# Casts, their remainders and the block differences of MLP 2 moved to other steps; the stores and weight sums of MLP 1 regrouped

## The chip, the cores and the metric

The kernel runs on one core of a Trainium2 chip. The metric is the device time of one execution in microseconds (us). The program has five instruction streams: TensorE (PE, with its weight loads shown apart as PEld), VectorE (DVE), ScalarE (ACT), GpSimd (POOL) and SyncE (SP). Each runs its own instructions strictly in their order; they meet at semaphores. A transfer is started by an instruction in one of these streams, and an instruction that waits there holds up all that stand behind it.

## The reference

```python
def reference(**kwargs):
    attn_out = _attn_ref(**attn_kwargs)      # 4 x 8 heads, 576 x 64, local and strided masks
    x = attn_out.transpose(0, 2, 1, 3).reshape(2304, 512)
    x = _moe_ref(x, w_in, w_out)             # MLP 1: h = x @ w_in; g = h * clip(h + 3, 0, 6) / 6; g @ w_out
    return _moe2_ref(x, w_in2, w_out2)       # MLP 2: h = x @ w_in2; g = max(h, 0) + log1p(exp(-|h|)); g @ w_out2
```

There are 2304 tokens of width 512, and the inner width of both MLPs is 2048. The weights come as float64.

## The kernel before, in words

**Numbers.** A float32 factor is split into a rounded part (`hi`, a cast by ACT) and the remainder (`lo`, a subtraction by DVE), both in the format that TensorE multiplies fast; a product is hi·hi + hi·lo + lo·hi, three matmuls. A block can't be multiplied before its cast and then its subtraction are done.

**Stages.** Attention is worked off in pieces beside MLP 1. MLP 1 runs over five chunks of tokens (`c`, one of 384 and four of 480) and 16 blocks of the inner width (`f`), 80 steps in all: `pe_h`, the activation on ACT and DVE (`post1`, `post2a`, `post2b`), and two steps later `pe_y`. At the end of a chunk `evac` copies four sums from PSUM into tiles `ysb` and stores them to `ydr` in DRAM (L781, L782). In chunk 0 the output weights are split and stored to `wdr` (`split_wout`, L151), and later chunks load them back (`load_split`, L157). The order of MLP 1's instructions is set by a scheduler.

**Preparing MLP 2's weights.** From chunk 1 on, each unit of four steps (16 units, numbered by `o` and `g`) loads two blocks of MLP 2's float64 weights (`prep_load`, one unit ahead), turns them into float32 (`w_scale` on ACT L116, `w_bits` on DVE L121 and L127), forms sums of blocks (`prep_sums`, DVE L198), splits the result (`prep_split`, ACT L216 and DVE L217 into tiles `so`, of which there are two) and stores it to `sdr` (L218): four casts, four subtractions and four stores per unit.

**MLP 2** multiplies 2 x 2 blocks with seven products in place of eight, so that sums and differences of blocks stand before and behind the products. It has three chunks of 768 tokens. A chunk has 56 steps of phase 1 (eight groups `g`, seven products `i` each, in a skewed order) and 56 of phase 2 (seven products in the order `ORDER2`, eight groups each); a step is six matmuls. The program order is the order written (`in_order()`); each step also issues one 256 KB weight load `su` (L859) on SP's queue, ten steps ahead. After a step of phase 1, `post_1` (L901 to L941) forms h on DVE (`vadd`, L866), the softplus on ACT (abs L932, exp L902, log L903) and its last step on DVE (`soft_end`, L897); two groups make a tile `gq`.

**The units of phase 2.** `t_unit(c, k)` makes one factor of phase 2 from a tile `gq`: for two of the seven products a block difference first (DVE L866, 768 columns), then the cast `th` (ACT L959) and the remainder `tl` (DVE L960). There are 28 units per chunk. Units 0 to 2 are written after the steps of product 2 of groups 3, 5 and 7 in phase 1, the others beside phase 2's steps, by the table `T_AT`; `X_AT` does the same for the next chunk's input (`x_split`, L821 and L822; `x_sums`, L810). `out_put` transposes a result on DVE (L970) before it is stored.

Of the kernel before, what the change touches and what calls it, by code (L numbers as in the profile page):

```python
# [7 lines left out]
F32 = mybir.dt.float32  # L8
# [8 lines left out]
P = 128  # L17
# [5 lines left out]
def attn_two_mlps(  # L23
# [120 lines left out]
    def split_wout(f):  # L144
        raw = words(1, 0, f, F32)[1]
        wst_t.pop((1, 0, f))
        hi, lo = sw_tile("woh"), sw_tile("wol")
        nc.scalar.copy(hi, raw)
        nc.vector.tensor_tensor(out=lo, in0=raw, in1=hi.bitcast(F32), op=ALU.subtract)
        for i, t in enumerate((hi, lo)):  # L150
            nc.sync.dma_start(out=wdr[f][i], in_=t.bitcast(F32))  # L151
        wo_t[0, f] = (hi, lo)
# [14 lines left out]

    def prep_f32(o, g):
        for f in (2 * g, 2 * g + 1):
            w_scale(o, 1, f)  # L170
        w_bits((o, 1, 2 * g), (o, 1, 2 * g + 1))

    def prep_parts(o, g, i):
# [8 lines left out]

    def prep_sums(o, g):
# [8 lines left out]
        for out_, x, y, op in (  # L192
            (s1, a21, a22, ALU.add),
            (s2, s1, a11, ALU.subtract),
            (s3, a11, a21, ALU.subtract),
            (s4, a12, s2, ALU.subtract),
        ):
            nc.vector.tensor_tensor(out=out_, in0=x, in1=y, op=op)  # L198

    def prep_split(o, g, i):  # L200
# [8 lines left out]
        for a, z, src in parts:  # L209
            t = wsl.tile([P, 2, 2, DH], F32R, tag="so", name="so")[:, : z - a]  # L210
            hi, lo = (t[:, :, j] for j in range(2))
            if o:
                hi, lo = (x.rearrange("p b (x m) -> p b m x", x=2) for x in (hi, lo))
                if a == 0:
                    src = src.rearrange("p b (m x) -> p b m x", x=2)
            nc.scalar.copy(hi, src)  # L216
            nc.vector.tensor_tensor(out=lo, in0=src, in1=hi.bitcast(F32), op=ALU.subtract)  # L217
            nc.sync.dma_start(  # L218
                out=sdr[o][g][4 * i + a : 4 * i + z].rearrange("b p n -> p b n"),
                in_=t.rearrange("p b j n -> p b (j n)").bitcast(F32),  # L220
            )
        wst_t.pop((o, 1, 2 * g + i))

# [641 lines left out]
    def vadd(out_, x, y, op=ALU.add):  # L865
        return nc.vector.tensor_tensor(out=out_, in0=x, in1=y, op=op)  # L866
# [80 lines left out]

    def t_unit(c, k):
        i, q = ORDER2[k // 4], k % 4
        g = g2_t[c, q]  # L950
        if i == 7:
            vadd(g[:, 0], g[:, 4], g[:, 0], ALU.subtract)
        elif i == 4:
            vadd(g[:, 1], g[:, 4], g[:, 1], ALU.subtract)
        hi, lo = (
            l2p["g"].tile([P, 2, HT], F32R, tag=f"t{n}", name=f"t{n}", bufs=5) for n in "hl"
        )
        raw = g[:, GI[i]]
        nc.scalar.copy(hi, raw)  # L959
        nc.vector.tensor_tensor(out=lo, in0=raw, in1=hi.bitcast(F32), op=ALU.subtract)  # L960
        tt[c, i, q] = (hi, lo)

# [37 lines left out]
    def pe2(step):  # L1000
# [14 lines left out]
        for mt in range(2):  # L1015
            for gg in range(NF2) if tail else [g]:
# [87 lines left out]
    with ExitStack():  # L1104
# [124 lines left out]
        for n, (l, c, f) in enumerate(seq):  # L1229
# [89 lines left out]
        X_AT = {  # L1319
            (5, 1): (0, 0), (5, 3): (1, 0), (5, 5): (0, None), (6, 1): (1, None),  # L1320
            (6, 3): (0, 1), (6, 5): (1, 1), (3, 3): (0, 2), (3, 5): (1, 2),
        }
        for k, step in enumerate(steps):
# [3 lines left out]
            with in_order():  # L1327
# [7 lines left out]
                for u in pre.pop(k, []):  # L1335
                    u()
                if post:
                    post()
                for u in aft.pop(k, []):
                    u()  # L1340
                if ph == 1:
                    if nxt is not None and g in (1, 2) and i == 1:
                        queue(1, x_load(nxt, g - 1))
                    if i == 2 and g % 2 and g > 2:
                        t_unit(c, g // 2 - 1)
                    if nxt is not None and i == 2 and g in (4, 6):
                        x_sums(nxt, g // 2 - 2, False)
                else:
                    for kk in T_AT.get((i, g), []):
                        t_unit(c, kk)  # L1350
                    if nxt is not None and (i, g) in X_AT:
                        kl, part = X_AT[i, g]
                        if part is None:
                            x_sums(nxt, kl, True)
                        else:
                            x_split(nxt, kl, part)
        with in_order():
# [69 lines left out]
```

## Time and profile before

| | |
|---|---|
| median of 3 runs | 927.65 us (924.52 to 933.07) |
| the profiled execution, its own time | 933.37 us |
| its span in the profile | 931.6 us |
| PE busy in the span | 91% |
| mean granted clock of TensorE | 0.954 |
| first to last matmul of MLP 2 | 507.67 to 923.30 us |

All times of the trace are of that one execution, and a sum of such times is to be taken from its 933.37 us; the runs lie around a median that is 5.7 us lower. PE is the engine with the most work. A granted clock of 1.00 is the level of 2.4 GHz and 0.50 that of 1.2 GHz.

### The profile page before, as it was taken

Reading aid. Unit: us, or ns where it says so; the run is one execution under the profiler, and the core shown is the slowest. Engines: PE = TensorE matmul, PEld = TensorE weight load, DVE = VectorE, ACT = ScalarE, POOL = GpSimd, SP = SyncE. Lnnn points to the kernel's source line nnn. Section 1 sums busy time; section 2 is a strip of 40 time slices with the busy share of each in tenths; the row PEclk is TensorE's granted clock in tenths of the full one; section 3 lists DMA queues with packets and bytes.
Section 4 is the critical chain, followed back from the end, with each engine's and each line's share of the span. In section 5 each row is a group of like instructions: output and inputs, shape, how many; then the busy total and the mean of one; then the engine's idle time right before and its main releaser. Section 6 shows DMA issues by size and latency. Waiting matters only on the chain.

```text
span 931.6 us, 17052 instructions
## 1 busy us (share of the span) xinstructions
PE 848.7 (91%) x6245; PEld 777.0 (83%) x6245; DVE 602.5 (65%) x1231; ACT 484.4 (52%) x978; POOL 7.6 (1%) x17
## 2 busy tenths in 40 slices
PE   4798899999989999999998987998987998978995
PEld 2698898878878888887887987998987998978995
DVE  5588876564566555656863476777656867565665
ACT  3478557443654465545543556632566622666430
POOL 3000000000000000000000000000000000000000
PEclk7699999999999999999999999999998999998998
DMA  8599999998789865967867876685995785975773
GB/s 238 150 338 226 321 343 312 212 325 274 242 242 282 266 224 174 259 215 256 271 217 254 294 222 197 205 249 157 300 326 174 231 253 164 303 225 177 248 242 68
DMA packets 181346, 225.44 MB, mean 242 GB/s; under 512 B 76432, under 2 KB 94224, under 8 KB 181264
## 3 DMA queue, kind: packets, MB, share of 16 engines
q1 hardware_dynamic: 179456, 223.38, 77.6%
q10 hardware_dynamic: 1808, 0.98, 0.4%
q8 instruction: 50, 0.82, 0.4%
q14 instruction: 32, 0.26, 0.1%
HBM read 177.08 MB, written 47.19 MB: 241 GB/s over the span
## 4 chain that ended last, share of the span: by engine, by line
PE 45%; DVE 17%; DMA 17%; ACT 13%; SPq 3%; issue 3%; ACTq 0%; DVEq 0%
PE psm L884 11%; PE psh L727 10%; PE psy L771 10%; PE psn L1024 8%; DMA wo<-in_w_out_dram 7%; PE psa L1024 5%; DVE gq L866 4%; DMA wi<-in_w_in_dram 4%; DVE tl L960 3%; DMA sdr<-so 3%; ACT th L959 2%; ACT sc L632 2%; ACT r L903 2%; ACT r L902 2%; DVE gq L897 2%
## 5 line engine op out<-in xcount | busy, mean ns | idle before, releaser
L884 PE MATMUL psm<-xh,su 128*128 128x384 f32 x672 | 182.9, 351 | 30.8 <-DVE u L866 26.4
L884 PEld LDWEIGHTS psm<-xh,su 128*128 128x128 f32 x672 | 129.1, 199 | 34.0 <-DVE u L866 29.3
L727 PE MATMUL psh<-xh,wih 128*128 128x480 f32 (+1 forms) x320 | 122.2, 382 | 6.8 <-DVE r L741 4.3
L1024 PE MATMUL psn<-th,su 128*128 128x384 f32 x480 | 127.3, 345 | 0.0
L727 PE MATMUL psh<-xl,wih 128*128 128x480 f32 (+1 forms) x320 | 120.9, 378 | 5.4 <-DVE xl L236 5.4
L771 PE MATMUL psy<-gh,woh 128*128 128x480 f32 (+1 forms) x320 | 121.1, 380 | 3.5 <-ACT ysb L781 2.4
L960 DVE TENSOR_TENSOR tl<-gq,th 128x768 fp32r<-128x768 f32 x84 | 78.7, 954 | 70.2 <-ACT th L959 70.1
L771 PE MATMUL psy<-gl,woh 128*128 128x480 f32 (+1 forms) x320 | 120.1, 375 | 1.2 <-DVE gl L754 1.0
L727 PE MATMUL psh<-xh,wil 128*128 128x480 f32 (+1 forms) x320 | 120.5, 377 | 0.1
L884 PE MATMUL psm<-xl,su 128*128 128x384 f32 x336 | 117.3, 349 | 0.0
L771 PE MATMUL psy<-gh,wol 128*128 128x480 f32 (+1 forms) x320 | 115.9, 373 | 0.0
L741 DVE SCALAR_TENSOR_TENSOR r<-r,psh 128x480 f32<-128x480 f32 (+1 forms) x80 | 50.2, 629 | 100.3 <-ACT r L740 100.2
L959 ACT CAST th<-gq 128x768 fp32r<-128x768 f32 x84 | 67.5, 833 | 69.9 <-DVE gq L866 52.3
L1024 PE MATMUL psn<-tl,su 128*128 128x384 f32 x240 | 83.9, 350 | 9.5 <-DVE tl L960 9.5
L1024 PEld LDWEIGHTS psn<-th,su 128*128 128x128 f32 x480 | 90.2, 194 | 0.0
L727 PEld LDWEIGHTS psh<-xh,wih 128*128 128x128 f32 x320 | 61.3, 192 | 15.6 <-DVE r L741 6.1
L727 PEld LDWEIGHTS psh<-xl,wih 128*128 128x128 f32 x320 | 61.4, 192 | 14.6 <-DVE xl L236 5.7
L932 ACT ACTIVATE r<-gq 128x384 f32<-128x384 f32 (+1 forms) x48 | 32.9, 684 | 77.8 <-DVE gq L866 77.6
L771 PEld LDWEIGHTS psy<-gh,woh 128*128 128x128 f32 x320 | 61.0, 191 | 12.7 <-ACT ysb L781 3.8
L727 PEld LDWEIGHTS psh<-xh,wil 128*128 128x128 f32 x320 | 61.4, 192 | 8.4 <-DVE wil L139 0.9
L771 PEld LDWEIGHTS psy<-gl,woh 128*128 128x128 f32 x320 | 61.2, 191 | 8.7 <-DVE gl L754 1.9
L748 ACT CAST gh<-r 128x480 fp32r<-128x480 f32 (+1 forms) x80 | 46.4, 581 | 41.8 <-DVE r L741 35.5
(135 smaller groups left out, 1364.1 us busy)
## 6 DMA issues: line engine op xcount, KB each, us to landing
su<-sdr SPq DMA_DIRECT2D x336, 256.0 KB
sdr<-so SPq DMA_DIRECT2D x48, 512.0 KB
wi<-in_w_in_dram SPq DMA_DIRECT2D x32, 512.0 KB
wo<-in_w_out_dram SPq DMA_DIRECT2D x32, 512.0 KB
woh<-wdr SPq DMA_DIRECT2D x64, 256.0 KB
wol<-wdr SPq DMA_DIRECT2D x64, 256.0 KB
wdr<-woh SPq DMA_DIRECT2D x16, 256.0 KB
wdr<-wol SPq DMA_DIRECT2D x16, 256.0 KB
```

Of the source, the lines that this page charges most:

```text
L632: nc.scalar.activation(out=s, in_=s, func=AF.Exp, scale=-1.0, bias=nm[:, pr, g, e : e + 1], accum_out=sm[:, pr, g, e : e + 1],)
L727: mark["PE"] = nc.tensor.matmul(ps[:, :n], lhsT=w[:, kt], rhs=x[:, :n], start=(kt == 0 and j == 0), stop=(kt == KT - 1 and j == 2),)
L741: mark["DVE"] = nc.vector.scalar_tensor_tensor(out=r, in0=r, scalar=6.0, in1=ps, op0=ALU.min, op1=ALU.mult)
L748: mark["ACT"] = nc.scalar.copy(hi, g32_t[l, c, f])
L771: mark["PE"] = nc.tensor.matmul(psy_t[l, c][m][:, :w], lhsT=a, rhs=bb, start=(f == 0 and j == 0), stop=(f == NF - 1 and j == 2),)
L866: return nc.vector.tensor_tensor(out=out_, in0=x, in1=y, op=op)
L884: nc.tensor.matmul(ps, lhsT=w[:, kl], rhs=x, start=i in (1, 5, 6) and kl == 0 and j == 0, stop=kl == 1 and j == 2, skip_group_check=True,)
L897: nc.vector.scalar_tensor_tensor(out=y, in0=x, scalar=0.0, in1=v, op0=ALU.max, op1=ALU.add)
L932: nc.scalar.activation(out=v, in_=x, func=AF.Abs)
L959: nc.scalar.copy(hi, raw)
L960: nc.vector.tensor_tensor(out=lo, in0=raw, in1=hi.bitcast(F32), op=ALU.subtract)
L1024: nc.tensor.matmul(psl[mt][:, :HT], lhsT=w[:, mt], rhs=x, start=i in (1, 4, 5, 6) and gg == 0 and j == 0, stop=gg == NF2 - 1 and j == 2, s ...
```

## The change

In MLP 1 all stores (`wdr`, `sdr`, `ydr`: 32, 64 and 20 transfers) go from SP's queue to GpSimd's. The tile `ysb` gets four buffers of 480 columns in place of two of 512. The preparation of a unit is cut into eight pieces, two per step: one ahead of `pe_y`, one behind it.

In MLP 2 `t_unit` is cut into `t_diff`, `t_cast` and `t_sub`. For units 0 to 2 the cast stands ahead of the post of product 3's step and the subtraction behind that post, one step of seven earlier than before. In phase 2 the cast of a unit stays at its step, or comes a step earlier, and its subtraction stands one step later; the block differences stand several steps ahead of their casts, and part of the next chunk's split moves to the last product's steps.

```diff
     def split_wout(f):
...
-            nc.sync.dma_start(out=wdr[f][i], in_=t.bitcast(F32))
+            nc.gpsimd.dma_start(out=wdr[f][i], in_=t.bitcast(F32))
...
-            nc.sync.dma_start(
+            nc.gpsimd.dma_start(
                 out=sdr[o][g][4 * i + a : 4 * i + z].rearrange("b p n -> p b n"),
...
+    def prep(n, h):
+
+        o, g = divmod(n, NF2)
+        if h == 0 and n + 1 < 2 * NF2:
+            prep_load(*divmod(n + 1, NF2))
+        if h < 2:
+            w_scale(o, 1, 2 * g + h)
+            w_bits((o, 1, 2 * g + h))
+        elif h < 4:
+            prep_sums(o, g, h - 2)
+        else:
+            prep_split(o, g, *divmod(h - 4, 2))
...
-        t = tp.tile([P, DM], F32, tag="ysb", name="ysb", bufs=2)
+        t = tp.tile([P, SB], F32, tag="ysb", name="ysb", bufs=4)
         nc.scalar.mul(t[:, :w], psy_t[l, c][m][:, :w], 1.0 / 6.0)
-        nc.sync.dma_start(out=ydr[c][m], in_=t[:, :w])
+        nc.gpsimd.dma_start(out=ydr[c][m], in_=t[:, :w])
...
-    def t_unit(c, k):
-        i, q = ORDER2[k // 4], k % 4
-        g = g2_t[c, q]
-        if i == 7:
-            vadd(g[:, 0], g[:, 4], g[:, 0], ALU.subtract)
-        elif i == 4:
-            vadd(g[:, 1], g[:, 4], g[:, 1], ALU.subtract)
...
+    def t_diff(c, i, q):
+        g, n = g2_t[c, q], GI[i]
+        vadd(g[:, n], g[:, 4], g[:, n], ALU.subtract)
+
+    def t_cast(c, k):
+        tt[c, k] = tuple(
             l2p["g"].tile([P, 2, HT], F32R, tag=f"t{n}", name=f"t{n}", bufs=5) for n in "hl"
         )
+        nc.scalar.copy(tt[c, k][0], t_raw(c, k))
+
+    def t_sub(c, k):
+        hi, lo = tt[c, k]
+        nc.vector.tensor_tensor(
+            out=lo, in0=t_raw(c, k), in1=hi.bitcast(F32), op=ALU.subtract
+        )
...
             post2b(l, c, f)
+            if c >= 1:
+                k, r = divmod(n - NF, 4)
+                with after("DVE"):
+                    prep(k, 2 * r)
             if n >= 2:
                 pe_y(*seq[n - 2])
...
-                    if r == 0:
-                        if k + 1 < 2 * NF2:
-                            prep_load(*divmod(k + 1, NF2))
-                        prep_f32(*unit)
-                    elif r == 1:
-                        prep_sums(*unit)
-                    else:
-                        prep_split(*unit, r - 2)
+                    prep(k, 2 * r + 1)
...
-        T_AT = {(1, 1): [3], (1, 2): [4], (1, 4): [5], (1, 5): [6], (1, 7): [7]}
-        for p, i in enumerate(ORDER2[1:-1], 1):
-            for g in range(0, NF2, 2):
-                T_AT[i, g] = [4 * p + g // 2 + 4]
...
+            for k, gc, gs in ((3, 0, 1), (4, 1, 2), (5, 3, 4), (6, 4, 5), (7, 6, 7)):
+                do(c, 1, gc, t_cast, c, k)
+                do(c, 1, gs, t_sub, c, k)
+            for k in range(8, 4 * len(ORDER2)):
+                p, q = divmod(k - 4, 4)
+                do(c, ORDER2[p], 2 * q, t_cast, c, k)
+                do(c, ORDER2[p], 2 * q + 1, t_sub, c, k)
+            for i, g, j, q in (
+                (5, 7, 7, 0), (6, 1, 7, 1), (6, 3, 7, 2), (2, 1, 7, 3),
+                (2, 3, 4, 0), (2, 5, 4, 1), (7, 1, 4, 2), (7, 3, 4, 3),
+            ):
+                do(c, i, g, t_diff, c, j, q)
+            if nxt is not None:
+                for i, g, kl, part in (
+                    (5, 2, 0, 0), (5, 4, 1, 0), (3, 1, 0, 2), (3, 3, 1, 2), (3, 5, 0, 1), (3, 6, 1, 1)
+                ):
+                    do(c, i, g, x_split, nxt, kl, part)
...
+                early = ph == 1 and i == 3 and g in (2, 4, 6)
+                if early:
+                    t_cast(c, g // 2 - 1)
                 if post:
                     post()
+                if early:
+                    t_sub(c, g // 2 - 1)
```

The order of TensorE's instructions in MLP 2 is the same. ACT's order changes around the third of the three early units; before, from the step of product 3 of group 5 to that of group 6 (L932, L902 and L903 are abs, exp and log, L910 the copy of product 1's sum, L959 the cast):

```order
L902 ACTIVATE r<-r 128x768
L903 ACTIVATE r<-r 128x768
L932 ACTIVATE r<-gq 128x768
L902 ACTIVATE r<-r 128x768
L903 ACTIVATE r<-r 128x768
L959 CAST th<-gq 128x768
L932 ACTIVATE r<-psm 128x384
L932 ACTIVATE r<-gq 128x384
```

After, where the same operations have the lines L939, L909, L910 and L966:

```order
L909 ACTIVATE r<-r 128x768
L910 ACTIVATE r<-r 128x768
L966 CAST th<-gq 128x768
L939 ACTIVATE r<-gq 128x768
L909 ACTIVATE r<-r 128x768
L910 ACTIVATE r<-r 128x768
L939 ACTIVATE r<-psm 128x384
L939 ACTIVATE r<-gq 128x384
```

The cast has moved ahead of one abs, exp and log of 768 columns; DVE's order at this place is unchanged.

On DVE, the steps of product 7 in phase 2 and the end of its results, before (L866 of 768 columns is a block difference, L960 a remainder, `u`, `cv` and `ot` belong to a result):

```order
L866 TENSOR_TENSOR gq<-gq 128x768
L960 TENSOR_TENSOR tl<-gq,th 128x768
L866 TENSOR_TENSOR gq<-gq 128x768
L960 TENSOR_TENSOR tl<-gq,th 128x768
L866 TENSOR_TENSOR u_7076<-s_6713,psn 128x384
L866 TENSOR_TENSOR cv<-u_7076,psn 128x384
L970 STREAM_TRANSPOSE ot<-cv 128x384
L866 TENSOR_TENSOR u_7082<-s_6715,psn 128x384
L866 TENSOR_TENSOR cv<-u_7082,psn 128x384
L970 STREAM_TRANSPOSE ot<-cv 128x384
L960 TENSOR_TENSOR tl<-gq,th 128x768 x4
```

After (a difference is L873, a remainder L970, a transpose L981):

```order
L970 TENSOR_TENSOR tl<-gq,th 128x768 x2
L873 TENSOR_TENSOR gq<-gq 128x768
L970 TENSOR_TENSOR tl<-gq,th 128x768
L873 TENSOR_TENSOR gq<-gq 128x768
L970 TENSOR_TENSOR tl<-gq,th 128x768
L873 TENSOR_TENSOR u_7071<-s_6716,psn 128x384
L873 TENSOR_TENSOR cv<-u_7071,psn 128x384
L981 STREAM_TRANSPOSE ot<-cv 128x384
L873 TENSOR_TENSOR u_7077<-s_6718,psn 128x384
L873 TENSOR_TENSOR cv<-u_7077,psn 128x384
L981 STREAM_TRANSPOSE ot<-cv 128x384
L970 TENSOR_TENSOR tl<-gq,th 128x768 x4
```

Before, each difference stands right ahead of the remainder whose cast reads it. After, the same difference stands ahead of another unit's remainder, and the fifth product's last remainder stands behind the `ot` of the results.

On SP, the loads of one unit's weights (`wi`) among the stores, in MLP 1's second chunk, before:

```order
L218 DMA sdr_2_118<-so 128x2x512
L157 DMA woh<-wdr_114 128x512
L157 DMA wol<-wdr_114 128x512
L218 DMA sdr_2_118<-so 128x2x512
L100 DMA wi_2700<-in_w_in_dram 128x512
L157 DMA woh<-wdr_115 128x512
L157 DMA wol<-wdr_115 128x512
L218 DMA sdr_2_118<-so 128x2x512
```

After:

```order
L157 DMA woh<-wdr_114 128x512
L157 DMA wol<-wdr_114 128x512
L100 DMA wi_2620<-in_w_in_dram 128x512
L157 DMA woh<-wdr_115 128x512
L157 DMA wol<-wdr_115 128x512
L100 DMA wi_2887<-in_w_in_dram 128x512
```

The stores are gone from SP's order there and stand in GpSimd's, which holds nothing else at that time.

## Rows read from the trace of the kernel before

**Rows 1.** Windows: us; busy PE, PEld, DVE, ACT, POOL; PE clock; DMA share; GB/s.

```profile
507.67:923.30 415.63, 375.41 (x2017) 368.36 (x2015) 278.99 (x404) 209.25 (x296) 0.00 (x0) 0.95 0.73 228
650.67:786.99 136.32, 124.37 (x674) 122.14 (x673) 96.53 (x141) 71.06 (x100) 0.00 (x0) 0.95 0.77 240
```

**Rows 2.** View of waits: who waited for whom, us in total, times, longest.

```profile
DVE tl L960 <- ACT th L959: 70.1, 49, 3.4
...
ACT so L216 <- DMA sdr<-so: 38.5, 24, 4.7
...
PE psm L884 <- DVE u L866: 26.4, 9, 3.6
...
PE psn L1024 <- DVE tl L960: 9.5, 9, 2.3
```

**Rows 3.** Timeline of PE in MLP 2: start, us, instruction [idle before it <-releaser].

```profile
514.29 0.44 PE L884 MATMUL psm<-xh,su 128*128 128x384 f32 x1 [4.36 <-ACT s L910]
...
681.35 0.44 PE L884 MATMUL psm<-xh,su 128*128 128x384 f32 x1 [2.59 <-DVE u L866]
...
706.37 0.33 PE L884 MATMUL psm<-xl,su 128*128 128x384 f32 x1
...
713.65 0.33 PE L884 MATMUL psm<-xl,su 128*128 128x384 f32 x1
...
717.79 0.69 PE L884 MATMUL psm<-xh,su 128*128 128x384 f32 x1 [3.62 <-DVE u L866]
...
776.96 0.44 PE L1024 MATMUL psn<-tl,su 128*128 128x384 f32 x1 [2.25 <-DVE tl L960]
```

**Rows 4.** Timelines of ACT and DVE before the stall that ends at 717.79.

```profile
712.96 0.85 ACT L932 ACTIVATE r<-gq 128x768 f32<-128x768 f32 x1 [2.50 <-DVE gq L866]
...
715.46 0.81 ACT L959 CAST th<-gq 128x768 fp32r<-128x768 f32 x1
...
716.31 0.96 DVE L960 TENSOR_TENSOR tl<-gq,th 128x768 fp32r<-128x768 f32 x1 [3.38 <-ACT th L959]
717.19 0.55 DVE L866 TENSOR_TENSOR u<-s,psm 128x384 f32<-128x384 f32 x1
```

**Rows 5.** Windows of the second chunk, columns as in rows 1.

```profile
682.06:685.47 3.41, 3.41 (x13) 3.41 (x12) 1.69 (x3) 2.40 (x4) 0.00 (x0) 0.50 0.98 350
716.20:723.03 6.83, 5.24 (x16) 5.24 (x17) 4.40 (x8) 3.08 (x6) 0.00 (x0) 0.50 0.16 51
...
697.78:707.00 9.22, 6.63 (x38) 6.63 (x39) 6.92 (x13) 5.81 (x10) 0.00 (x0) 1.00 0.56 177
```

**Rows 6.** Timelines of ACT and DVE at the end of phase 2's fifth product.

```profile
770.44 3.78 ACT L959 CAST th<-gq 128x768 fp32r<-128x768 f32 x5 [1.97 <-DVE gq L866]
...
771.31 0.96 DVE L960 TENSOR_TENSOR tl<-gq,th 128x768 fp32r<-128x768 f32 x1 [0.98 <-ACT th L959]
...
775.97 2.65 DVE L960 TENSOR_TENSOR tl<-gq,th 128x768 fp32r<-128x768 f32 x3
```

**Rows 7.** Timeline of ACT where MLP 1 passes into MLP 2.

```profile
512.66 1.20 ACT L781 ACTIVATE ysb<-psy 128x480 f32<-128x480 f32 x2 [5.06 <-DMA ydr<-ysb]
```

**Rows 8.** Timelines of SP, ACT and PE in MLP 1.

```profile
251.90 0.75 SPq L100 DMA_DIRECT2D wi<-in_w_in_dram x1
...
258.56 0.67 ACT L116 ACTIVATE wi<-wi 128x512 f32<-128x512 f32 x1 [4.23 <-DMA wi<-in_w_in_dram]
...
265.49 0.66 PE L727 MATMUL psh<-xh,wih 128*128 128x480 f32 x1 [2.46 <-DVE r L741]
...
434.32 0.48 PE L771 MATMUL psy<-gh,woh 128*128 128x480 f32 x1 [1.72 <-ACT ysb L781]
```

**Rows 9.** Timelines of DVE and ACT: a weight unit's remainders, the next cast.

```profile
496.12 1.62 DVE L217 TENSOR_TENSOR so<-wo,so 128x512 fp32r<-128x512 f32 x2
...
500.28 1.13 ACT L216 CAST so<-wo 128x512 fp32r<-128x512 f32 x1 [3.45 <-DMA sdr<-so]
```

**Rows 10.** SP's own waits: who for whom, us in total, times, longest.

```profile
SPq L218 <- DVE so L217: 97.8, 36, 9.8
```

More of the change, by code (lines that the diff above doesn't have):

```diff
@@ L166, in prep_load @@
             (load_wout if o else load_win)(1, f)
[L168 to L171, printed above, removed]
     def prep_parts(o, g, i):
@@ L181, in prep_parts, with prep_sums @@
         return ev, od
-    def prep_sums(o, g):
+    def prep_sums(o, g, part):
         (e0, d0), (e1, d1) = (prep_parts(o, g, i) for i in range(2))
@@ L196, in prep_sums, with prep_split @@
             (s4, a12, s2, ALU.subtract),
-        ):
+        )[2 * part : 2 * part + 2]:
             nc.vector.tensor_tensor(out=out_, in0=x, in1=y, op=op)
-    def prep_split(o, g, i):
+    def prep_split(o, g, i, part):
         ev, od = prep_parts(o, g, i)
@@ L208, in prep_split @@
             parts = [(0, 2, ev), (3, 4, od[:, 1:])]
-        for a, z, src in parts:
+        for a, z, src in parts[part : part + 1]:
             t = wsl.tile([P, 2, 2, DH], F32R, tag="so", name="so")[:, : z - a]
@@ L221, in prep_split @@
             )
-        wst_t.pop((o, 1, 2 * g + i))
+    def prep(n, h):
[9 more added lines that the diff above has]
+            prep_split(o, g, *divmod(h - 4, 2))
     x_t = {}
@@ L313, in loc_b_post1 @@
         if bp:
-            s = tp.tile([P, DM], F32, tag="ysb", name="s", bufs=2)
+            s = tp.tile([P, SB], F32, tag="ysb", name="s", bufs=4)
         else:
@@ L946, in attn_two_mlps, with t_raw @@
     GI = {1: 0, 2: 1, 3: 2, 5: 3, 6: 4, 7: 0, 4: 1}
-    def t_unit(c, k):
-        i, q = ORDER2[k // 4], k % 4
-        g = g2_t[c, q]
-        if i == 7:
-            vadd(g[:, 0], g[:, 4], g[:, 0], ALU.subtract)
-        elif i == 4:
-            vadd(g[:, 1], g[:, 4], g[:, 1], ALU.subtract)
-        hi, lo = (
+    def t_raw(c, k):
+        return g2_t[c, k % 4][:, GI[ORDER2[k // 4]]]
+    def t_diff(c, i, q):
[3 more added lines that the diff above has]
+        tt[c, k] = tuple(
             l2p["g"].tile([P, 2, HT], F32R, tag=f"t{n}", name=f"t{n}", bufs=5) for n in "hl"
         )
[L958 to L961, printed above, removed]
+        nc.scalar.copy(tt[c, k][0], t_raw(c, k))
[4 more added lines that the diff above has]
+        )
     out_rows = out.rearrange("c t n -> (c t) n")
@@ L1021, in pe2 @@
                 )
-                th, tl = (t[:, gg % 2] for t in tt[c, i, gg // 2])
+                th, tl = (t[:, gg % 2] for t in tt[c, ORDER2.index(i) * 4 + gg // 2])
                 for j, (w, x) in enumerate(((hi, th), (hi, tl), (lo, th))):
@@ L1273, in attn_two_mlps @@
                 k, r = divmod(n - NF, 4)
-                unit = divmod(k, NF2)
                 with after("DVE"):
-                    if r == 0:
-                        if k + 1 < 2 * NF2:
-                            prep_load(*divmod(k + 1, NF2))
-                        prep_f32(*unit)
-                    elif r == 1:
-                        prep_sums(*unit)
-                    else:
-                        prep_split(*unit, r - 2)
+                    prep(k, 2 * r + 1)
             if last1 and f >= 1:
@@ L1313, in attn_two_mlps, with do @@
         l2p["r"] = ctx.enter_context(tc.tile_pool(name="l2r", bufs=2, side="right", reuse_waits="tile"))
-        T_AT = {(1, 1): [3], (1, 2): [4], (1, 4): [5], (1, 5): [6], (1, 7): [7]}
-        for p, i in enumerate(ORDER2[1:-1], 1):
-            for g in range(0, NF2, 2):
-                T_AT[i, g] = [4 * p + g // 2 + 4]
[L1319 to L1322, printed above, removed]
+        at = {}
+        def do(c, i, g, fn, *a):
+            at.setdefault((c, i, g), []).append(lambda: fn(*a))
+        for n, c in enumerate(CHS):
+            nxt = CHS[n + 1] if n + 1 < NCH else None
+            for k, gc, gs in ((3, 0, 1), (4, 1, 2), (5, 3, 4), (6, 4, 5), (7, 6, 7)):
[15 more added lines that the diff above has]
+                    do(c, i, g, x_split, nxt, kl, part)
+                for kl in range(2):
+                    do(c, 6, 5 + 2 * kl, x_sums, nxt, kl, True)
         for k, step in enumerate(steps):
@@ L1343, in attn_two_mlps @@
                         queue(1, x_load(nxt, g - 1))
-                    if i == 2 and g % 2 and g > 2:
-                        t_unit(c, g // 2 - 1)
                     if nxt is not None and i == 2 and g in (4, 6):
@@ L1348, in attn_two_mlps @@
                 else:
[L1349 to L1356, printed above, removed]
+                    for u in at.get((c, i, g), []):
+                        u()
         with in_order():
```

## The prediction

> **What bounds the kernel now.** I read the page first: PE is busy 91% of the span and its mean granted clock is 0.954, so time can only come from where PE stands idle or runs at the lower level. The windows then split the span: MLP 2 takes 415.63 us from its first to its last matmul, with PE busy 375.41 of them at a clock of 0.95 [rows 1]. What would it take without a stop? In the timeline of PE two like rows, 706.37 and 713.65, have 42 matmuls between their starts, 0.173 us each [rows 3]. A chunk has 112 steps of six matmuls, 672 x 0.173 = 116.5 us, three chunks 349. The second chunk takes 136.32. So MLP 2 holds at most 415.6 - 349 = 66 us, and no edit of it can give more.
>
> Where the 66 lie is told by the waits on PE's side [rows 2]: 26.4 us in nine stops of phase 1 for DVE's `u`, 9.5 us in nine stops of phase 2 for DVE's `tl`, and one of 4.36 us at the passage from MLP 1 for ACT's copy [rows 3]. Together 40.3. The rest is clock: after such stops the granted clock is 0.50 for a while. In the second chunk three spells: 3.41 us behind the first stop, 6.83 behind the third, of which PE is busy 5.24, and one like the first near the chunk's end, whereas none follows the second stop of 2.59 us (clock 1.00 from 697.78 to 707.00) [rows 5]. A matmul takes twice as long in them, so half the busy time is lost: (3.41 + 5.24 + 3.41) / 2 = 6.0 us a chunk, 18.1 for three, and 1.7 for one more spell behind the passage. Stops and clock make 60 of the 66.
>
> **Phase 1, stops 1 to 3 of each chunk (2.59, 2.59 and 3.62 us).** All three have one form, and the third shows it [rows 4]. ACT stands idle for 2.50 us until 712.96, then does abs, exp and log, and casts only at 715.46. DVE's remainder waits 3.38 us for that cast and starts at 716.31; behind it in DVE's queue stands `u`, which PE needs. PE has nothing wrong with its own inputs: it waits for an instruction that is queued behind a waiting one. The change puts the cast ahead of the abs. Its 0.81 us fit into ACT's idle 2.50 (from 710.46, done near 711.3), since the block that it reads is older than the one the abs waits for; abs, exp and log start no later than now, so nobody behind the cast pays. At 712.96 DVE has done what stands ahead of the remainder (that released the abs). Then: remainder at 712.96, `u` 0.88 later as today (716.31 to 717.19), done at 713.84 + 0.55 = 714.39. PE stopped at 717.79 - 3.62 = 714.17. So about 0.3 us stay of the third stop; I take 0.5. The first two are one step (1.04 us) shorter, which is the slack that they would have: zero. Gain 26.4 - 1.5 = **24.9 us**.
>
> **Phase 2, end of the fifth product (9.5 us).** Today difference, cast and remainder of a unit are a chain across two engines: the cast waits 1.97 us for DVE's difference, then the remainder 0.98 us for the cast [rows 6]. A difference is a vector pass over 768 columns like the remainder, so 0.96 + 0.81 + 0.96 = 2.7 us per unit [rows 4], against two steps of PE, 2.08: the units fall behind by 0.7 each, and the results (`u`, `cv`, `ot`), queued behind them, start late; the next product's first remainder, at 775.97, comes 2.25 us late for PE [rows 3, 6]. With the differences some steps ahead only 2 x 0.96 = 1.9 us of DVE per two steps is left, and no wait between engines. The new order puts the unit's last remainder behind the results. These take 3.8 us on DVE (from 771.31 + 0.88 = 772.2 to 775.97), so from the start T of the sixth product's first step: that remainder is done at T + 4.8, needed six steps on, T + 6.2; the next at T + 5.7, needed at T + 8.3. In the last chunk two more transposes crowd this place; I leave 0.7 us, most of one vector operation. Gain 9.5 - 0.7 = **8.8 us**. The moved splits of the next chunk's input lie on ACT and DVE in steps with no casts; I cost them at nothing, bounds 0 to 1 us a chunk.
>
> **The passage (4.36 us).** ACT's third and fourth `ysb` wait 5.06 us for the first two tiles' stores [rows 7], and PE's copy stands behind them. With four buffers nothing waits there: the wait began at 512.66 - 5.06 = 507.60; from there the second pair, 1.2 us, and the copy, some 0.5, are done near 509.4, and PE needs it at 514.29 - 4.36 = 509.93. Gain **4.4 us**.
>
> **Clock.** If no stop over 0.5 us is left, the spells behind them go: **19.8 us**. The row after 697.78 shows a longer stop without a spell, so a rest of 0.5 should not bring one.
>
> **MLP 1.** Two of its stops touch what is changed [rows 8]: 1.72 us for `ysb`, and 2.46 us before 265.49, some us after ACT had waited 4.23 us for a weight load which SP had issued only at 251.90, between stores on which SP waits for DVE, 97.8 us in all [rows 10]. With the stores off SP the loads go out earlier. Both stops together are 4.2 us, and with a spell like the short ones behind the second (1.7) some 6. Against it stands what no row shows: stores by GpSimd. Bounds: a gain of 6 if both go, and a loss of 6 if the new order of the pieces makes two more like them. I take **4**, as the row at 251.90 names the cause.
>
> The Trainium skill speaks against this term ("DMA: Bandwidth & Descriptors", section "Issuing engines are not separate DMA queues"): transfers run on the same 16 DMA engines whoever starts them, and another issuer saves only the time of starting. By that rule the term would be 0 and the time 4 us longer; the rows of SP's waits speak for more, since what SP loses there is not starting but standing behind a store.
>
> **Sum.** 24.9 + 8.8 + 4.4 + 19.8 + 4 = 61.9. Against the profiled execution's own time: 933.4 - 61.9 = 871.5. The median of the runs is 5.7 lower than that execution: 927.65 - 61.9 = **866**.
>
> **Rivals.**
> (A) The third stop of phase 1 stays. The reckoning leaves it 0.3 us late, so a small slip on DVE (one vector operation of 0.55 to 0.96 queued ahead) makes it 1 to 2 us, and then its long spell of clock stays as well: 3 x (2 + 2.6) = 14 us given back, **880**. For it: there is no reserve. Against: ACT has 71 of 136 us busy and DVE 96 [rows 1], so lag doesn't pile up. If phase 2 slips too, 890.
> (B) GpSimd's stores are slow, and the time ends on the other side. The tile `so` has two buffers and four pieces per unit. A unit is four steps of 24 matmuls of 480 columns (0.173 x 480 / 384 = 0.217 us each), 20.8 us; a buffer is used twice in it, each time 1.1 us of cast, 1.1 of remainder and the store's time L. Up to 2 x (2.2 + L) = 20.8, L = 8.2 us, ACT catches up within the unit; beyond it each of 16 units costs 2 x (L - 8.2). It eats the 62 us at L = 10.1: there it decides, and at L = 11 the time is 955. Nearest row: under SP, the first of two remainders that begin at 496.12 is done about 497.2 and its buffer is free at 500.28 [rows 9], L = 3.1. ACT already waits 38.5 us for such stores with no loss in proportion [rows 2]. So L would have to triple.
> (C) DMA becomes the bound of MLP 2: now a share of 0.73 at 228 GB/s [rows 1], it would be 0.73 x 415.6 / 358 = 0.85; and a window of the trace moved 350 GB/s [rows 5]. Unlikely; 880.
> (D) The change doesn't do what it says: the block that the early cast reads is not ready, ACT waits there ahead of the abs and the stops stay. Then only passage and MLP 1 gain: 927.65 - 10 = 918, or 927 if those fail too.
>
> A rule of the Trainium skill bears on (B) ("SBUF — State Buffer", section "SBUF: two separate sides", the trap that DVE blocks DMA): while DVE runs in one of its two-port modes, GpSimd can't write the descriptors of its own transfers. No run so far shows a store by GpSimd. By it a store here could wait for one such operation at a time, which is why I give (B) 0.06 in all and not 0.03.
>
> **Chances.** Forecast (856 to 875) 0.73; (A) 0.14; (C) 0.03; (B) with a part of the gain left, 870 to 915, 0.03, and slower 0.03; (D) 0.04, half of it within 1%. A measurement of this kernel tells a change from none at about 1%. Faster by over 1%: 0.94; within 1%: 0.03; slower by over 1%: 0.03. Range: low end 853 (all of the 66 and MLP 1's 6 would give 856, less the spread of the runs); high end 884, which takes in most of (A) and (C).
>
> **What the profile after would show.** MLP 2 in about 358 us, chunks of about 118 to 119; no wait of PE for `u` over 0.6 us and none for `tl` over 0.8; casts of the early units in ACT's idle time ahead of an abs; a clock of 1.00 through MLP 2; no wait of `ysb` for `ydr`; SP's wait for `so` gone, and on ACT a wait for `sdr` no longer than 4.7 us. Wrong would be: spells of 0.50 with hardly a stop ahead of them, new waits for `su`, or long waits of ACT at `so` and, behind them, of PE in MLP 1.

## The result, and the profile after

The changed kernel takes 872.84 us (870.45 to 875.19, four runs) against 928.84 us (924.52 to 933.07, four runs): a ratio of 0.940, 95% interval 0.935 to 0.945. The forecast was 866 in a range of 853 to 884. The profiled executions, 933.37 and 870.45 us, lie 62.9 apart, the medians 56.0: by chance the one of before was the slowest of its four and the one of after the fastest.

The windows over MLP 2, first matmul to last, and over its second chunk, answer to [rows 1]:

```profile
506.33:860.43 354.10, 350.95 (x2017) 349.22 (x2015) 276.30 (x404) 208.75 (x296) 2.07 (x4) 1.00 0.84 268
624.20:742.00 117.80, 115.76 (x666) 115.12 (x666) 94.75 (x139) 71.05 (x100) 0.00 (x0) 1.00 0.86 274
```

MLP 2 went from 415.6 to 354.1 us, with a clock of 1.00 throughout: no spell of 0.50 is left in it. MLP 1 begins to pass into it at 506.33 where it was 507.67. So of the 62.9 us between the two executions 61.5 are MLP 2's and 1.3 lie before it.

The view of waits, beside [rows 2]:

```profile
POOL sdr L213 <- DVE so L212: 279.1, 47, 17.3
...
ACT wi L116 <- DMA wi<-in_w_in_dram: 45.3, 16, 10.7
...
DVE so L212 <- ACT so L211: 37.3, 21, 5.9
ACT so L211 <- DMA sdr<-so: 26.7, 19, 4.6
...
DVE tl L970 <- ACT th L966: 8.5, 8, 2.2
...
PE psm L891 <- DVE u L873: 3.1, 4, 1.3
```

PE's wait for `u` fell from 26.4 us in nine stops to 3.1 in four, and its wait for `tl` is gone. DVE's wait for the casts `th` fell from 70.1 to 8.5. In MLP 1 two rows became worse: ACT waits 45.3 us for the weights `wi`, and DVE waits 37.3 us for ACT's casts at `so`. Before they were 39.1 and 18.1:

```profile
ACT wi L116 <- DMA wi<-in_w_in_dram: 39.1, 17, 11.2
...
DVE so L217 <- ACT so L216: 18.1, 13, 4.6
```

PE's stops in MLP 2 are these, all of them, against the nine, nine and one of [rows 2, 3]:

```profile
563.23 0.44 PE L891 MATMUL psm<-xh,su 128*128 128x384 f32 x1 [0.56 <-DVE u L873]
...
660.53 0.45 PE L891 MATMUL psm<-xh,su 128*128 128x384 f32 x1 [1.33 <-DVE u L873]
...
682.34 0.45 PE L891 MATMUL psm<-xh,su 128*128 128x384 f32 x1 [0.71 <-DVE u L873]
...
799.67 0.44 PE L891 MATMUL psm<-xh,su 128*128 128x384 f32 x1 [0.55 <-DVE u L873]
```

Three of them are what is left of the third stop of each chunk. The timelines of ACT and DVE before 682.34 show the place of [rows 4] as it is now:

```profile
678.46 0.82 ACT L966 CAST th<-gq 128x768 fp32r<-128x768 f32 x1
680.99 0.85 ACT L939 ACTIVATE r<-gq 128x768 f32<-128x768 f32 x1 [1.71 <-DVE gq L873]
...
680.87 0.95 DVE L970 TENSOR_TENSOR tl<-gq,th 128x768 fp32r<-128x768 f32 x1
681.74 0.54 DVE L873 TENSOR_TENSOR u<-s,psm 128x384 f32<-128x384 f32 x1
```

The cast runs in ACT's idle time, the abs starts behind it as soon as its input is there, and the remainder starts with no wait; `u` follows it and is 0.7 us late. The stop of 1.33 us has another cause, which DVE's timeline names: a sum for the next chunk's input, ahead of `u` in the queue, waits for that input's transfer.

```profile
659.45 0.56 DVE L817 TENSOR_TENSOR xr<-xr 128x384 f32<-128x384 f32 x1 [1.84 <-DMA xr<-ydr]
659.93 0.55 DVE L873 TENSOR_TENSOR u<-s,psm 128x384 f32<-128x384 f32 x1
```

At the passage the four copies `ysb` run without a break and the copy that PE needs comes at 507.58, with no stop of PE (compare [rows 7]):

```profile
505.23 1.96 ACT L788 ACTIVATE ysb<-psy 128x480 f32<-128x480 f32 x4 [1.80 <-PE psy L778]
507.58 0.48 ACT L917 COPY s<-psm 128x384 f32<-128x384 f32 x1 [0.39 <-PE psm L891]
```

### The profile page after: what moved, and what is told of

The parts are those of the page before. It is cut to its first block, busy times and chain, and to the rows that moved or that the text cites. A ratio compares the mean times of both kernels' runs of the same rounds, so it can differ in the third digit from the quotient of the medians.

```text
span 868.7 us, 17121 instructions
## 1 busy us (share of the span) xinstructions
PE 824.6 (95%) x6245; PEld 758.0 (87%) x6245; DVE 601.1 (69%) x1231; ACT 483.1 (56%) x978; POOL 81.1 (9%) x133
## 4 chain that ended last, share of the span: by engine, by line
PE 51%; DMA 15%; issue 14%; DVE 10%; ACT 7%; SPq 1%; POOL 1%; POOLq 0%; DVEq 0%; ACTq 0%
PE psn L1035 14%; PE psm L891 11%; PE psy L778 9%; PE psh L734 9%; DMA sdr<-so 7%; PE psa L1035 6%; DMA wi<-in_w_in_dram 3%; DVE gq L873 2%; DVE so L212 2%; DVE gq L904 2%; DMA wo<-in_w_out_dram 2%; ACT so L211 1%; SPq L515 1%; ACT r L910 1%; ACT r L939 1%
## 5 line engine op out<-in xcount | busy, mean ns | idle before, releaser
L891 PE MATMUL psm<-xh,su 128*128 128x384 f32 x672 | 172.2, 335 | 3.1 <-DVE u L873 3.1
L891 PEld LDWEIGHTS psm<-xh,su 128*128 128x128 f32 x672 | 121.4, 188 | 4.5 <-DVE u L873 4.4
L1035 PE MATMUL psn<-th,su 128*128 128x384 f32 x480 | 123.1, 335 | 0.0
L891 PE MATMUL psm<-xl,su 128*128 128x384 f32 x336 | 112.3, 334 | 0.0
L966 ACT CAST th<-gq 128x768 fp32r<-128x768 f32 x84 | 68.8, 834 | 67.1 <-PE psn L1035 43.6
L1035 PEld LDWEIGHTS psn<-th,su 128*128 128x128 f32 x480 | 86.8, 188 | 0.0
L970 DVE TENSOR_TENSOR tl<-gq,th 128x768 fp32r<-128x768 f32 x84 | 77.6, 949 | 8.5 <-ACT th L966 8.5
L1035 PE MATMUL psn<-tl,su 128*128 128x384 f32 x240 | 80.5, 335 | 0.0
L213 POOL DMA_DIRECT2D sdr<-so x64 | 44.4, 696 | 294.6 <-DVE so L212 279.1
```

The source lines that it names most:

```text
L213: nc.gpsimd.dma_start(out=sdr[o][g][4 * i + a : 4 * i + z].rearrange("b p n -> p b n"), in_=t.rearrange("p b j n -> p b (j n)").bitcast(F32),)
L891: nc.tensor.matmul(ps, lhsT=w[:, kl], rhs=x, start=i in (1, 5, 6) and kl == 0 and j == 0, stop=kl == 1 and j == 2, skip_group_check=True,)
L966: nc.scalar.copy(tt[c, k][0], t_raw(c, k))
L970: nc.vector.tensor_tensor(out=lo, in0=t_raw(c, k), in1=hi.bitcast(F32), op=ALU.subtract)
L1035: nc.tensor.matmul(psl[mt][:, :HT], lhsT=w[:, mt], rhs=x, start=i in (1, 4, 5, 6) and gg == 0 and j == 0, stop=gg == NF2 - 1 and j == 2, s ...
```

## The experiments

Theory: MLP 2's new order gives nearly all, MLP 1's part the passage and little else. The rival gives MLP 1's stores on another queue a gain of their own. Times are medians; ratios are to the kernel before on the same chip. Runs of one kernel scatter by half a per cent and more. As far as the profiles show, most of that arises in MLP 1: the kernel below with MLP 1's part alone has the same instructions in MLP 1 as the changed kernel, and MLP 2 began at 511.3 us in its profile and at 506.3 in the other; in the two kernels at the end that split MLP 2's part, again with this MLP 1, it began at 505.8 and 511.8. So gains of MLP 2 are read from its stretch in the traces, and those of MLP 1 from ratios.

**MLP 2's part alone.** MLP 1 as before.

```diff
-        t = tp.tile([P, SB], F32, tag="ysb", name="ysb", bufs=4)
+        t = tp.tile([P, DM], F32, tag="ysb", name="ysb", bufs=2)
...
-        nc.gpsimd.dma_start(out=ydr[c][m], in_=t[:, :w])
+        nc.sync.dma_start(out=ydr[c][m], in_=t[:, :w])
```

and so for the other stores and the pieces.

> Only the part of the change in MLP 2; MLP 1 as before (stores by SP, two ysb tiles, four pieces per unit). Theory 1: nearly all of the gain is MLP 2's new places for casts, remainders and differences, and of MLP 1's part only the passage counts (a stop of 4.4 us and a spell of clock worth 1.7). Then the time is 872.8 + 6 = 879 us, the stop at the passage is there, and the nine stops for u and the nine for tl come to under 4 us in all. Theory 2: the stores off SP give some 4 to 5 us in MLP 1 besides: 884. Theory 3: MLP 2's part alone gives little, since the stores free SP for the weight loads: over 900.

Measured: 878.04 us, ratio 0.940 (0.937 to 0.944). That is the ratio of the whole change, within the intervals. PE's stops for `u` are 3.5 us and there is none for `tl`; the stop at the passage is there:

```profile
513.20 0.45 PE L884 MATMUL psm<-xh,su 128*128 128x384 f32 x1 [3.70 <-ACT s L910]
```

So MLP 1's part as a whole brings nothing that a measurement shows, though it removes this stop.

**MLP 1's part alone.** MLP 2 as before (`t_unit` and its table are back).

```diff
-                early = ph == 1 and i == 3 and g in (2, 4, 6)
...
+                    if i == 2 and g % 2 and g > 2:
+                        t_unit(c, g // 2 - 1)
```

> Only the part of the change in MLP 1; MLP 2 as before. Theory 1: the passage and a us or so: 928.8 - 7 = 922 us, MLP 2's stops for u still 26.4 us, for tl 9.5. Theory 2 (MLP 1 gains some 4 to 5 us by itself): 917. Theory 3: under 900.

Measured: 927.92 us, ratio 0.998 (0.995 to 1.001). That is a gain of 1.9 us (-1 to 5 by the interval), less than either theory said, and the passage by itself should give 6 (its stop of 4.4 and its spell of 1.7). So something in this part must cost most of what the passage gives.

**All stores on SP's queue again**, tiles and pieces as in the change.

```diff
-            nc.gpsimd.dma_start(
+            nc.sync.dma_start(
                 out=sdr[o][g][4 * i + a : 4 * i + z].rearrange("b p n -> p b n"),
```

and so for `wdr` and `ydr`.

> The changed kernel with all stores back on SP's queue (four ysb tiles and eight pieces per unit stay). Theory 1: no difference that a measurement shows, 872 to 875 us. Theory 2 (the stores off SP give 4 to 5 us): 877 to 878, and SP's wait for DVE at the stores is some 98 us again, with ACT's waits for weight loads and PE's stops behind them longer than in the changed kernel.

Measured: 864.37 us, ratio 0.927 (0.924 to 0.930). Both theories are refuted: the stores off SP neither gain nor are neutral, they cost some 1.2%, 8 to 12 us. MLP 2's stretch is the same (354.1 us), so the loss is in MLP 1. Of the 8 to 12 us the two profiles show 4.2, by the time at which MLP 2 begins (506.3 against 502.1). Its view of waits shows where it differs from the changed kernel:

```profile
ACT wi L116 <- DMA wi<-in_w_in_dram: 39.0, 18, 10.3
...
ACT so L211 <- DMA sdr<-so: 31.7, 21, 3.7
...
DVE so L212 <- ACT so L211: 11.5, 12, 3.6
```

DVE's wait at `so` is 11.5 us where GpSimd's stores make it 37.3.

**Two `ysb` tiles**, the rest as in the change.

```diff
-        t = tp.tile([P, SB], F32, tag="ysb", name="ysb", bufs=4)
+        t = tp.tile([P, SB], F32, tag="ysb", name="ysb", bufs=2)
```

> The changed kernel with two ysb tiles in place of four. Theory 1: the stop at the passage is back at 4 to 5 us for ACT's copy, with a spell of 0.50 behind it: 872.8 + 6 = 879 us. Rival: on GpSimd's queue nothing stands ahead of these stores, so the tiles come free sooner and the stop is under 3 us, with or without a spell: 874 to 876.

Measured: 887.92 us, ratio 0.950 (0.946 to 0.955). That is 1.1% or 10 us more than the change, and so more than the 6 us of the passage. The stop there is 5.2 us for ACT's copy.

**Four `ysb` tiles alone**, and then **eight pieces alone**, each with the changed MLP 2 and all stores on SP. Of the change in MLP 1 the first keeps only

```diff
-        t = tp.tile([P, DM], F32, tag="ysb", name="ysb", bufs=2)
+        t = tp.tile([P, SB], F32, tag="ysb", name="ysb", bufs=4)
```

and the second only

```diff
-                        prep_split(*unit, r - 2)
+                    prep(k, 2 * r + 1)
```

with the function `prep` and its other call.

> The changed MLP 2, and of MLP 1's part only the four ysb tiles; stores by SP, four pieces per unit. Since all stores on SP gave 864 (0.927 of before) where the change has 873 (0.940), and MLP 2's part alone 878 (0.940 on its chip), the ysb tiles and the pieces are worth some 12 us together and GpSimd's queue costs some 8 to 11. Theory 1: the tiles are worth the passage, 6 us, and the stops for ysb at the other chunk ends, 2 to 3 us: ratio 0.931 to 0.934. Theory 2: the pieces carry the 12 us: ratio 0.937 to 0.940.

> The changed MLP 2, and of MLP 1's part only the eight pieces per unit; stores by SP, two ysb tiles. Theory 1 (the tiles carry most): ratio 0.936 to 0.939, with the stop at the passage still 4 to 5 us. Theory 2 (the pieces carry it): 0.929 to 0.932.

Measured: the tiles 862.99 us, ratio 0.930 (0.926 to 0.934); the pieces 875.93, ratio 0.942 (0.938 to 0.947). MLP 2's part alone has 0.940. So the tiles carry the gain, about 1.1% or 10 us, and the pieces nothing that shows. The passage is 3.7 + 1.7 of the 10; PE's stops at L771 for `ysb` at the chunk ends in MLP 1, 3.2 us in four in the kernel with MLP 2's part alone, are gone too. The rest isn't assigned.

**Only `wdr` on GpSimd's queue**, and then **only `sdr`**; the rest as in the change. The first puts back

```diff
-            nc.gpsimd.dma_start(
+            nc.sync.dma_start(
                 out=sdr[o][g][4 * i + a : 4 * i + z].rearrange("b p n -> p b n"),
```

the second

```diff
-            nc.gpsimd.dma_start(out=wdr[f][i], in_=t.bitcast(F32))
+            nc.sync.dma_start(out=wdr[f][i], in_=t.bitcast(F32))
```

and both the store to `ydr`.

> The changed kernel with only chunk 0's 32 stores to wdr on GpSimd's queue; those to sdr and ydr on SP's. Theory A: GpSimd's queue costs in chunk 0, where the DMA engines are full (share 1.0 from 80 to 150 us) and stores that no longer wait in SP's order compete with the weight loads: then this is as slow as the change, ratio 0.936 to 0.940, and steps 16 to 20 of MLP 1 end some 3 us later than with SP. Theory B: it costs at sdr, by later release of the tiles so: then 0.927 to 0.930 here.

> The changed kernel with only the 64 stores to sdr on GpSimd's queue; those to wdr and ydr on SP's. Theory A (the cost lies in chunk 0): ratio 0.927 to 0.930. Theory B (it lies at sdr: 5.4 us from issue to landing on GpSimd's queue, two tiles so): 0.936 to 0.940, with ACT's waits at so longer than the 31.7 us that the kernel with all stores on SP shows. Theory C: neither alone, but ydr (GpSimd's copies behind long waits for sdr's remainders): both this and the kernel with wdr alone at 0.927 to 0.930.

Measured: `wdr` alone 865.02 us, ratio 0.931 (0.926 to 0.936); `sdr` alone 869.36, ratio 0.937 (0.932 to 0.941); none 0.927, all 0.940. Most of the cost is at `sdr` (theory B); the `wdr` part can't be told from nothing. The profiles agree: with four `ysb` tiles MLP 2 begins at 505.8 to 511.8 us in five kernels with `sdr` on GpSimd's queue, and at 496.6 to 502.8 in four with it on SP's. DVE's wait at `so` is 11.4 us with `wdr` alone and 36.9 with `sdr` alone. An episode of the kernel with `sdr` alone, in the timelines of DVE, POOL and ACT:

```profile
236.78 1.29 DVE L212 TENSOR_TENSOR so<-wi,so 128x512 fp32r<-128x512 f32 x2
...
238.10 1.45 POOL L213 DMA_DIRECT2D sdr<-so  x2 [15.03 <-DVE so L212]
...
243.69 0.65 ACT L211 CAST so<-wi 128x512 fp32r<-128x512 f32 x1 [0.52 <-DMA sdr<-so]
...
244.38 0.69 DVE L212 TENSOR_TENSOR so<-wi,so 128x512 fp32r<-128x512 f32 x1 [3.33 <-ACT so L211]
244.99 0.65 DVE L748 SCALAR_TENSOR_TENSOR r<-r,psh 128x480 f32<-128x480 f32 x1
```

Two remainders end near 237.4 and 238.1. POOL starts the two stores in 1.45 us, and the first tile is free only at 243.69, some 6.3 us after its remainder; under SP it was 3.1 [rows 9]. DVE stands 3.33 us at the next remainder, and behind it stands `r`, which MLP 1's next product needs: the same form as the stops of MLP 2. PE has no stop here, but later in the same trace the chain reaches it:

```profile
466.48 2.19 ACT L211 CAST so<-wo 128x512 fp32r<-128x512 f32 x2 [1.80 <-DMA sdr<-so]
...
467.62 2.18 DVE L212 TENSOR_TENSOR so<-wo,so 128x512 fp32r<-128x512 f32 x2 [4.57 <-ACT so L211]
469.64 0.65 DVE L748 SCALAR_TENSOR_TENSOR r<-r,psh 128x480 f32<-128x480 f32 x1
...
470.34 0.48 PE L734 MATMUL psh<-xh,wih 128*128 128x480 f32 x1 [1.31 <-DVE r L748]
```

The three longer stops for `r` of this kernel (2.32, 2.21 and 1.86 us) have an attention transfer, a weight load and the next input's sums ahead of `r`, not a tile `so`. So the chain is shown for one stop, and not for the whole loss. On PE's side the loss can be seen in the last third of MLP 1: from 350 to 500 us PE is busy 143.1 us with `sdr` alone on GpSimd's queue, and 148.3 with all stores on SP.

```profile
350.00:500.00 150.00, 143.08 (x904) 121.58 (x903) 91.90 (x173) 74.37 (x139) 18.32 (x26) 0.99 0.72 229
350.00:500.00 150.00, 148.32 (x941) 127.55 (x940) 95.23 (x183) 77.22 (x142) 0.00 (x0) 1.00 0.71 230
```

The page of the changed kernel, in its part on issues, gives a median of 5.4 us from issue to landing for these stores (for SP's queue the pages give none):

```profile
sdr<-so POOLq DMA_DIRECT2D x48, 512.0 KB, 5.4
```

**Three tiles `so`**, with two `ysb` for room and all stores on GpSimd.

```diff
-            t = wsl.tile([P, 2, 2, DH], F32R, tag="so", name="so")[:, : z - a]
+            t = wsl.tile([P, 2, 2, DH], F32R, tag="so", name="so", bufs=3)[:, : z - a]
```

> The changed kernel with all stores on GpSimd's queue, two ysb tiles (the room that this frees is needed) and three tiles so in place of two. To be held against the kernel with two ysb tiles and two tiles so on GpSimd's queue (ratio 0.950) and against the same two and two with stores on SP (0.942). Theory 1: GpSimd's stores cost by the late release of so (a free tile comes 4 to 8 us after its remainder is done, with SP's stores from 2.9 us on): a third tile takes that wait away, ratio 0.940 to 0.943, and DVE's wait for ACT's cast at so falls from 39 us to under 18. Theory 2: they cost in another way (competition of the transfers, GpSimd's port): ratio stays 0.948 to 0.952.

Measured: 878.33 us, ratio 0.945 (0.943 to 0.948). It lies between the two theories: by the medians it gives back some two thirds of the way from 0.950 with two tiles (0.946 to 0.955) to the 0.942 of stores on SP (0.938 to 0.947), and its interval overlaps both. DVE's wait at `so` fell from 38.9 us to that of theory 1:

```profile
DVE so L212 <- ACT so L211: 17.9, 7, 4.4
```

So the late release of `so` is a part of what GpSimd's stores cost, by the medians the larger one; how large, and what the rest is, stays open.

**Phase 1's early casts with phase 2 as before**, and then **phase 2's new order with units 0 to 2 as before**, one run each.

```diff
+                j = ORDER2[k // 4]
+                if j in (7, 4):
+                    do(c, ORDER2[p], 2 * q, t_diff, c, j, k % 4)
                 do(c, ORDER2[p], 2 * q, t_cast, c, k)
-                do(c, ORDER2[p], 2 * q + 1, t_sub, c, k)
...
+                do(c, ORDER2[p], 2 * q, t_sub, c, k)
```

and so for units 3 to 7 and the next chunk's split.

> The changed kernel with phase 2 of MLP 2 in the order of before (difference, cast and remainder of a unit at one step); the early casts of units 0 to 2 stay. Theory: the two parts add. Phase 2's nine stops for tl (9.5 us) and a spell of 0.50 a chunk (1.7 each) are back, the stops for u stay at 3 us: MLP 2 from first to last matmul 353.8 + 9 + 5 = 368 us. Rival: phase 2's stops came from lag that phase 1 passed on, so that the early casts alone remove them: 354 to 357 us.

```diff
-                if early:
-                    t_cast(c, g // 2 - 1)
                 if post:
                     post()
-                if early:
-                    t_sub(c, g // 2 - 1)
                 for u in aft.pop(k, []):
                     u()
+                if ph == 1 and i == 2 and g % 2 and g > 2:
+                    t_cast(c, g // 2 - 1)
+                    t_sub(c, g // 2 - 1)
```

> The changed kernel with units 0 to 2 of MLP 2 cast where they were before; phase 2's new order stays. Theory: the stops for u are back (26.4 us in place of 3.2), with two spells of 0.50 a chunk worth 4.3 us: MLP 2 takes 353.8 + 23.2 + 13 = 390 us, and no stop for tl over 0.8 us. Rival (the parts need each other): over 395, with stops for tl.

Measured: windows over MLP 2 of the first,

```profile
505.80:880.62 374.82, 359.72 (x2017) 354.29 (x2015) 277.66 (x404) 207.39 (x296) 2.07 (x4) 0.98 0.80 252
```

and of the second:

```profile
511.78:902.93 391.15, 364.74 (x2017) 361.41 (x2015) 277.35 (x404) 210.96 (x296) 2.07 (x4) 0.97 0.77 243
```

The second is as expected: it takes 391.2 us, PE's wait for `u` is 26.4 us in nine stops again, and none for `tl`. The first has 10.2 us of stops for `tl` as expected, but takes 374.8 and not 368: one stop for `u`, at the input's sum in the second chunk, grew to 3.56 us, and a spell of 0.50 of 6.83 us followed it. Undoing one part alone costs 20.7 and 37.1 us; with the passage (6.1 by its terms) that makes 63.9, close to the 61.5 of the whole. So the two parts add, to within some 2 us.

**Stores on SP, and two more moves in MLP 2**: the early sums of the next input go to phase 2, and the third unit's remainder behind the last `u`.

```diff
+                    do(c, 1, 3 + 2 * kl, x_sums, nxt, kl, False)
...
-                if early:
+                if early and g < 6:
                     t_sub(c, g // 2 - 1)
+                if ph == 1 and i == 7 and g == 7:
+                    t_sub(c, 2)
...
-                    if nxt is not None and i == 2 and g in (4, 6):
-                        x_sums(nxt, g // 2 - 2, False)
```

> The changed kernel with all stores on SP's queue, and in MLP 2 the early sums of the next chunk's input moved from phase 1 to phase 2 (they waited for the input's transfer with u queued behind them) and the third unit's remainder moved behind u of the last group. Theory: the four stops for u that the changed kernel has left (0.56, 1.33, 0.71, 0.55 us) go, MLP 2 takes 350.6 us; the time is that of the kernel with all stores on SP, 864.4 (0.927), less 3: 861, ratio 0.923 to 0.927. Rival: the remainder or the sums come late in phase 2 and PE waits there for tl: 864 or more.

Measured: 861.57 us, ratio 0.926 (0.924 to 0.929), the best of all. By time it can't be told from the kernel with all stores on SP (0.927), but PE has no stop for `u` left in MLP 2, and two of 0.2 us for `tl`; the stretch is 1.4 us shorter:

```profile
496.61:849.27 352.66, 352.22 (x2017) 349.72 (x2015) 275.90 (x404) 208.83 (x296) 0.00 (x0) 1.00 0.85 269
```

Both kernels, before and changed, are beaten by it.

## Why the prediction was right, and where it was not

**Phase 1.** Right in mechanism and size. The casts run in ACT's idle time, the first two stops of each chunk are gone, and the third is 0.55 to 0.71 us where 0.5 was taken. The stop of 1.33 us for the input's transfer was not seen.

**Phase 2.** Right: with the differences ahead no stop for `tl` is left, not even the 0.7 us allowed. With the old order back they were 10.2 us.

**The passage.** Right for the stop. But stop and spell are only about half of what the four tiles give, 10 us in all.

**Clock.** Right: 1.00 through MLP 2. The sum for MLP 2 was 57.9 and its stretch lost 61.5. The prediction had left 6 of the 66 us unassigned; now 354.1 - 349.4 = 4.7 us are left above the unstopped time, 3.1 of them stops, so most of the 6 went together with stops and clock; no row says what they were.

**MLP 1's term, 4 us: this step failed in its reason and its sign.** The reason given was that weight loads wait in SP's queue behind the stores, and that one such load made the stop of 2.46 us before 265.49 [rows 8]. The rows of DVE there say otherwise: `r` stands right behind a transpose of attention's keys, which waited for their transfer.

```profile
263.69 1.26 DVE L554 STREAM_TRANSPOSE kT<-sk 128x576 f32<-128x576 f32 x1 [1.15 <-DMA sk<-in_ks_dram]
264.79 0.64 DVE L741 SCALAR_TENSOR_TENSOR r<-r,psh 128x480 f32<-128x480 f32 x1
```

In the changed kernel ACT scales its `wi` at 257.00 without a wait, and the stop is still there, with the same transpose ahead of `r`:

```profile
258.61 1.26 DVE L561 STREAM_TRANSPOSE kT<-sk 128x576 f32<-128x576 f32 x1 [1.47 <-DMA sk<-in_ks_dram]
259.71 0.64 DVE L748 SCALAR_TENSOR_TENSOR r<-r,psh 128x480 f32<-128x480 f32 x1
...
260.40 0.49 PE L734 MATMUL psh<-xh,wih 128*128 128x480 f32 x1 [1.86 <-DVE r L748]
```

Nor did ACT's waits for `wi` fall in all: 45.3 us with the stores gone, and 39.0 with them back on SP. As to size, the traces show 1.3 us for MLP 1. MLP 1's part alone gains 1.9 by ratio, with the passage's 6 in it, so that the rest of MLP 1 lost about 4 (1 to 7 by the interval) where a gain of 4 was forecast; in its profile MLP 2 begins 3.6 us later than before. Behind that are two effects: the tiles give some 4 to 5 us beyond the passage, and GpSimd's queue takes 8 to 12.

**Rival (B)** was the right place and the wrong price. It set a threshold at L = 8.2 us, below which ACT was to catch up within a unit. In the episodes shown L rose from about 3 to about 6, and the stores to `sdr` cost most of the 8 to 12 us (0.937 against 0.927). The reckoning took the mean over a unit of 20.8 us, but the four splits of a unit stand in two of its four steps, so that a tile is wanted again after some 5 us (an estimate: a quarter of the 20.8). In the trace of before the shortest distance between two casts into the same tile is 5.5 us; with `sdr` alone on GpSimd's queue it is 7.1. And while DVE waits at a remainder its later instructions wait too. The rule of issuing engines that was cited ("DMA: Bandwidth & Descriptors", section "Issuing engines are not separate DMA queues", the Trainium skill) put the term at 0. That is nearer than the forecast's gain of 4, but the queue alone is no zero, as the run with stores on SP shows: it costs 8 to 12 us. Whether GpSimd's descriptors waited for DVE, as the other cited rule would have it ("SBUF — State Buffer", section "SBUF: two separate sides", the Trainium skill), no run here tells; GpSimd's own instruction took 0.57 to 0.89 us in all 64 stores to `sdr` of the kernel with these alone on its queue.

**Rivals (A), (C) and (D)** did not come true: the third stop is the 0.55 to 0.71 us above, the DMA share rose to the 0.84 that (C) reckoned with no wait of PE for `su`, and all nine early casts start without a wait for their blocks.

**The sum.** 61.9 us by the working, 62.9 between the profiled executions, 56.0 between the medians: the time forecast was 7 us too low against the median, and most of that is the difference between the profiled executions and the medians, which the working had set at 5.7 for before and had no value for after. That 61.9 came so near 62.9 is partly luck: MLP 2 gave 3.6 more than its terms, MLP 1 2.7 less than its own, and the two executions were the slowest and the fastest runs of their kernels.

## What to carry to other kernels

When an engine stops for something short, look at what stands ahead of that instruction in its engine's queue: here three casts a chunk, moved ahead of instructions that they had no need to follow, were worth 37 of the 61.5 us, since they had been holding DVE and with it PE. Moving stores to an idle engine's queue was not free: the time until a buffer could be used again about doubled, and with two buffers that was a wait on the engines that fill them. And a stop should be followed back through the queue of the engine that ended it before a cause is named: the load at 251.90 was near the stop of 2.46 us, but DVE's queue names another wait. A group of edits should be measured one by one: here four tiles gained 10 us, the queue lost as much, and together they looked like nothing.

## What was not expected of the hardware

In the episodes shown the same kind of store took about twice as long to free its tile from GpSimd's queue as from SP's (about 6 us against 3), with some 0.7 us of POOL's time for each.

The length of a stop does not by itself tell whether the clock falls. In the kernel with MLP 2's part alone the stop of 2.07 us before 667.73 was followed by a spell of 0.50:

```profile
668.18:671.59 3.41, 3.41 (x12) 3.41 (x12) 2.44 (x4) 3.19 (x5) 0.00 (x0) 0.50 1.05 380
```

In the kernel with all stores on SP one of 2.32 us, before 260.56, was not:

```profile
260.56:270.00 9.44, 9.44 (x48) 8.26 (x49) 7.68 (x15) 4.79 (x9) 0.00 (x0) 1.00 0.96 263
```

At the same place of the program a shorter stop was, in the changed kernel, the 1.86 us before 260.40:

```profile
261.02:264.43 3.41, 3.41 (x10) 2.82 (x9) 2.87 (x7) 1.27 (x3) 0.00 (x0) 0.50 0.82 176
```
